# Transposes grouped, layer 2's products regrouped, and a new written-out order, in a kernel of attention and two feed-forward layers

## The chip, the cores and the metric

One core of one Trainium2 chip runs the whole kernel. The metric is device time in microseconds (us) of one execution; lower is better. Engine names are those of the profile: PE is TensorE's matmul, PEld its weight load, DVE VectorE, ACT ScalarE, POOL GpSimd, and SP the SyncE queue, which here issues all DMAs.

## What is computed

The reference, cut to its core:

```python
q, k, v: (4, 8, 576, 64) fp32;  w_in: (512, 2048), w_out: (2048, 512), twice, fp64
q_d, k_d, v_d = means over 4 neighbouring tokens of q, k, v
out_up  = repeat(softmax(q_d @ k_d.T / 8) @ v_d, 4 times along tokens)
scores  = where(|i - j| < 4, q @ k.T / 8, -1e9)
x = (out_up + softmax(scores) @ v)  reshaped to (2304, 512)
h = x @ moe_w_in;   x = (h * sigmoid(h)) @ moe_w_out
h = x @ moe2_w_in;  out = (h * sigmoid(1.702 * h)) @ moe2_w_out
```

## The kernel before

The two feed-forward layers are most of the work. Weights and activations are split into a high and a low fp16 half, and each matrix product is the sum of three products of halves. The weights come from memory as fp64 in 1 MB and 0.5 MB pieces and are converted on the way: ACT (L323, L327, L344), DVE (L331, L336, L348) and for some pieces POOL (L348) put the bits together, a sum on PE with ones (L557) and DVE reductions give a common scale, and ACT (L376, high half) and DVE (L380, low half) write the fp16 halves.

**Attention** runs in 32 units: 8 half batches m of 288 tokens, 4 pairs of heads each. A unit needs k and q with the head dimension on partitions, and their means over 4 tokens. For half batches 0 and 1 both are made on PE: for every 96 tokens `keys_of.tr` (L1128, L1129; once per batch and head pair, six chunks) and `unit.qtr` (L1173, L1174; once per unit, three chunks) issue a transpose (96 columns) and a product with the matrix `four` (24 columns, the means). That is 4 calls of 6 pairs and 8 calls of 3 pairs, 48 pairs. The other half batches use DVE for it. Then come the scores (L1198 pooled, L1204 local), the softmax on DVE, ACT and POOL (L1212 to L1256), the product with v (L1280, L1286), ACT's copy `us` (L1292) and DVE's addition into `xf` (L1300, L1301), which frees the PSUM banks of the product for the next use.

**Layer 1** takes 288 tokens at a time (L702 up, L819 and L847 down). **Layer 2** takes nine tiles of 256 tokens. A tile has eight steps p = 0 to 7 (gate pairs), each with 24 matmuls of 256 columns (L881) and, behind it, tanh on ACT (L893), a multiplication on DVE (L896), three sums (L900 to L902, on DVE or POOL), the high half on ACT (L906) and the low half on DVE (L909). Then 168 matmuls (L960) form seven products of sums of g and sums of weights. `PARTS` cuts each product into ranges of p: a part (product, p0, p1) issues three matmuls for each p, and needs both halves of g of its last p.

**What sets the order.** The code adds 2663 steps to a plan, each with its engine and what it depends on. `PLACES`, a string of two digits per step, gives each step a place, `Plan.placed` sorts by it, and each engine, and the DMA queue, issues its steps in that order. `ON` names the steps that go to another engine than their usual one: conversion steps (`sg`, `cp`), the softmax's subtraction, normalisation and division (`LS`, `LN`, `DN`), and layer 2's three sums (`gs2.tile.p`).

Of the kernel before, what the change touches and what calls it, by code (L numbers as in the profile page):

```python
# [36 lines left out]
def on(name, usual):  # L37
# [12 lines left out]
    "2l2x2B2p2F2I2K2L2O2R2S2W353d3n3h444w66828A2n1X2V3S2P2U2X37313c383b3k3m3u3r3v3K3H3O3X4041333f3j3y3t3D3z3J3L3P3T42464d4n4v4C4N5K43474b4i"  # L50
    "4m4o4r4y4B4H4O4R545g5h5m5w5z5C4Q4X505b5c5i5k5o5q5s5y5x5F5H5E5L5U5W5X63656A6Z768sai2G3E6148324u7s4U527B8b6f7d8o6r5R3Q3V4j5f5l5Y6n6b6s6o"
    "6x6z6B6H6F6J6T6P7e7n7t9k494c5B5N5Q6D6X6L776Y7l7v7C7M7J7N7Z7W81878c8z5T6g8j6V7w7z7P7L7U8d8f8m8n8u8r8x8H8F8K8Q8T927S7Y8O7p7x8h8B8l8D8q8v"
    "8I8L8N8R8W908X9497989b9p9u9y9Cac9FeM72858J9v8G939a9h9f9l9i9o9G9J9O9K9S9Wa9abafalbM8V8Z9w9Q9N9Z9R9Va3a5a8a7aqaCaNaOaTb1bV9maoasaAavaKaz"
    "aQaSaUaWb0b5bcaXbvbGbKbOaxaEb3b6bjb9brbtbwbybAbCbPbRbNbUbXbYbZc3c9cbchcPeoja6Q9Eag9n7XcCd3aMaFcYe9bLbxdmcHboaDbnbEb4bic0c6c5cac7cccfcg"
    "cjcmcDcOcxcVd7d9fCbqcucUbebgcycFcIcKcNcQcTcXdId6djdldLdQdUdXe3bscMdfcwczdgdqdudHdvdKdNe4e5eaedele7eCeGeIfscicldEcZd2e6egerenevexezeAeB"
    "eEeLePeDeTeXeZf0fJfNfPfTg8hXm5dceue0fbdAdCf1f4f6f9fafdfefgflfqfwfzfofYg5gcgZf8fufvfBfEfGfHfMfSfUfVfZgggjgmgEh0h3jhg0g3gfghgqgzgwgBgGgN"
    "h6gPhHhKhxhWi2i5i8gTgXh8hkhihMhmhnhPhThZi9ieihibikiuiwiMjujyjAjPjRkMjEdsfhg6gdejifgSh1gKjzitiXfRkGiWkHj4fFfKhoilioiyiDiEiLiIiJiQiRjliZ"
    "jijOk8kakgkhm1fxiVjrhrhvjejmjIjWjLjMk1k3k7ktkxkIkNl1lbldlehtjZkwj9jbkrkDkykOkPkWkYkZlWlmlwlAlYm6mdmemJl4lhlXkmkvlplGlslLlvlJlOlSlUm2mi"
    "mlmhmmmomqmLmNmVngnknMogrrjGkqlTlFkTkUmvmxmEmzmKmRmUn4njndnrnLnDnTo3odpRlulInnnsnynNnEnVnXokoqonozoKotoRoYp5qln3o7ofowouoDoEoHoJoOp6oU"
    "papopeprpPpTq9oQoTp8pbpfpkpjpqpsptpVpFpXq0q8qbqfqhqiqmqsqtqvqGquqw393w3M3Y4E4J3F3W4a4f4l4T4k4A4K4P4V4Z4F4S5d5j5p5v575e5r5G5P685t5S646l"  # L60
    "6v7k6e6k6C6G898e6t6w6I6S7G7R6O6W7f71797o7i7r7A7E7I807O7V8i868a8t8k8p8C8y8E8M8P8Y95999c9L969d9q9t9x9A9j9r9z9D9Haa9B9I9P9T9Ya19M9Ua2a6ay"
    "aHa0a4adajamapaeakaratawbaauaBaIaLaVb8aGaJaPb2cncJaRaYbubzbDddb7bbbhbpbBbHbQbWc1c4c8ceckcpcscGcLcScRcWd5dedhdwd4dadidndOdSdkdtdydDdFdR"
    "dxdBdMdPebepdGdJdWe1efekdTe2e8eceYf2eeemeteweReVeqeyeQfffih7eFeNeWf3f7fcfjfrgpfyfDfLfQg4gagigrgygxgAgHgRgUhhgLgQh2h5hchfgWh4h9hdhuhEhb"
    "hghlhphshYhjhqhyhAhDiihwhChIhLhQhUhJhNi0i3ivj0hSi1imiHjwjFi7igisiBiGiNiUj1jcj6j8jjjojvjBjJjNjSjQjTjVjXk0kijUjYk6k9kokQk4keklkpkKl0kjkz"
    "kFkJkRlgkEkLkVl2lBlCkSkXl3l7l9lql6lalillmYnflfljlHlRmDmHlrlylElKlQlVm0m3m8mcmjmnmsmwmCmImMmPmOmSn2n7nbnBn0n6nhnmnInQncninqnwnCo0ntnAnH"
    "nJocoenGnKnSnZo1opnOnYo4o5o8oBo2o6ohojoIoMoboioSoZpmqaomoroAoGoLoWp3pcpppipnpvpzpDpHpKpOq2pUpZq5q6qgqkq4q7qcqdqpqyqeqjqoqqqCqOqnqrqBqD"
    "qKqMqAqEqIqLqRqUqJqNqQqSqVr4qPqTr1r6rDrJqZr5rGrLrTswrbrfrjrorurxrCrKrPrNrVs1s6s7sascsgslsjspstsusxsDsssvsEsGsJsNsCsIsMsPsQsSsLsOsUsXsY"
    "tcsRsVt1t2t9tesZt3t6tatdtht5tbtgtltptttwtytDtAtEtGtItKtNtQtTtY6p8g91aZbdbfblbm8U9s9e9XahbkcobJ8S9gbSctbTd0dbdpbFcdc2cqcrcvcAcBanbId8dV"
    "dzdZeHesd1dodreJeieOeUeScEeKehfkf5fIg7fOdYfmfAftfWg1gCgnfpgbfXgkgegogugvfng9glgFgtgJgYhag2gOgDhzgVhBhOhFgsgMi6hViaidizijgIhei4hRiniriP"
    "iAhGipiCiFiKiOjdiSiciTixj3j2j5jtjDiqiYjfjgjkjnjxjqjsjKk2kdkcknkulPj7jCjpjHkbkfkskkkAl8lcm7ltmbmfmgkClkl5lnlolzlNlDmkmtmrmumymBmFmGmamp"  # L70
    "mQn1n5n9nenulMmTmWmXmZnlnznpmAnxoanRolosoxoyn8nFnonUnPnWoNoCnanvp0p4p7p9pxpdoooFoPoVoXp2pLphpgpypupBpApEpJq1plpIpMpNpQpSrhpWp1pwpGqXr3"
    "r7r9raq3rgrkrnrmrwryrzpYrerdrirlrsrArBkBqxqzqWr2ovqFqHr0rqlxqYr8rcrMk5rprtrvrHrErFrIrOrQrRrSs8sis9sbrZsHsKtftorXsTt4sWt0rWtitrtntJrUsd"
    "sosqt7tOtRueulsntutztMtPtStWu7ubtstBtFtHtLtVtZu0u3t8tqtvtxtCu2u6uZv3tUm9rYs0s2s3s5sesksBpCs4sfshsyvcvesAszm4smsrtjtkwcwYtmu9lZsFuYv7vq"
    "y2yqyswIo9v9vavkvmxZzEzwwuvnvpwewHy9zZBlBnCsx0x2xQyvzyBdBhA3DQvryazmzCzDChE3A2CJybB3DkF8FaFcFhFgFftXu1u5uaugumuqu4u8udufuiupusucuhukuo"
    "uwuAuGujunutuvuxuEuHuruuuzuBuDuKuTuyuCuIuLuOuSuWuFuJuNuPuRuVv0uMuQuXv1v5v8vduUv2v4v6vbvfvhvgvjvivlvovtvsvuvwvvvxvzvyvKvMvAvBvNx6vCvDvF"
    "vGvIvPvTvEvHvLvOvRvVw0vJvQvUvWvYw2w7vSvXw1w3w5w9whvZw4w8wawdwiwlw6wbwgwjwnwqwvwfwkwowpwswwwywmwrwxwzwBwDwFwtwAwCwEwGwJwLwKwNwMwOwPwRwQ"
    "wSwUwTwVwXwWx3x5wZx1xayWx4x7x9xbxdxgxlx8xcxfxhxjxnxsxexixmxoxqxuxzxkxpxtxvxxxBxHxrxwxAxCxExIxLxyxDxGxJxOxRxVxFxKxNxPxTxWxYxMxSxXy0y3y5"
    "y7xUy1y4y6y8ycyeydygyfyhyiykyjylytymynypyoyRyVyryuzfAaywyxyzyAyCyKyNyyyByEyFyHyXz0yDyGyJyLyPyTyYyIyMyQyUz2z9zdyOySz3z4z8zizoyZz1z5z7za"
    "zczgz6zbzhzkzlzpzrzezjzqzszuzxzAznztzvzzzBzFzHzGzJzIzKzLzNzMzOA4zPzQzSzRA6A8zTzUAOAQzVzWzYA0A5AcAgzXA1A9AbAeAiAnA7AdAhAjAlApAuAfAkAoAq"
    "AsAwACAmArAvAxAzADAGAtAyABAEAJAMARAAAFAIAKANASAUAHALATAVAXAZB1APAWAYB0B2B4B6B5B8B7B9BaBcBbBeBgBfBiBkBjCiClBmBoBtDIBpBqBsBuBwBzBEBrBvBy"  # L80
    "BABCBGBLBxBBBFBHBJBNBSBDBIBMBOBQBUC0BKBPBTBVBXC1C4BRBWBZC2C7CaCdBYC3C6C8CbCeCgC5C9CfCkCmCoCqCcCjCnCpCrCtCvCuCxCwCyCzCBCACCDECDCECGCFCI"
# [1438 lines left out]
```

## Time and profile before

| | |
|---|---|
| three runs | 901.15, 902.54, 902.81 us; median 902.54 |
| profiled execution | 902.26 us, of which the span is 900.5 us |
| PE busy | 864.3 us (96% of the span) |
| PEld busy | 717.7 us (80%) |
| DVE busy | 623.0 us (69%) |
| ACT busy | 464.0 us (52%) |
| POOL busy | 150.3 us (17%) |
| mean granted clock | 0.996 |

The profile shows one execution. Busy time counts what an engine spends in instructions; its idle time is put down to the releaser that came last. 1.76 us of the execution's own time lie outside the span. Line numbers are those of the kernel before; in the changed kernel the same lines stand up to 5 further on.

### The profile page before, as it was taken

How to read it: one execution, taken by the hardware profiler on the slowest of the kernel's cores; microseconds unless marked ns; L12 is line 12 of the kernel's file. 1: busy time of each engine (PE TensorE's matmuls, PEld its weight loads, DVE VectorE, ACT ScalarE, POOL GpSimd, SP SyncE). 2: the span in 40 equal slices, each digit the busy share in tenths (PEclk: the TensorE clock that was granted, in tenths of full speed). 3: DMA queues.
4: the chain of work that ended last, by engine and by line, in shares of the span. 5: the costliest groups of instructions: out<-in, count | busy, mean ns of one | idle time of the engine just before them, and what ended most of it. 6: DMA issues, size and time to landing. Idle time of an engine off the chain costs nothing.

```text
span 900.5 us, 23832 instructions
## 1 busy us (share of the span) xinstructions
PE 864.3 (96%) x10212; PEld 717.7 (80%) x10212; DVE 623.0 (69%) x1365; ACT 464.0 (52%) x820; POOL 150.3 (17%) x165
## 2 busy tenths in 40 slices
...
GB/s 269 204 241 230 190 63 113 69 89 127 120 118 155 150 104 98 121 106 84 129 13 293 66 41 1 12 1 24 1 25 1 36 1 13 1 36 1 25 13 36
DMA packets 116190, 77.04 MB, mean 86 GB/s; under 512 B 94836, under 2 KB 101492, under 8 KB 115060
## 3 DMA queue, kind: packets, MB, share of 16 engines
...
## 4 chain that ended last, share of the span: by engine, by line
PE 66%; DVE 25%; ACT 4%; issue 2%; DMA 2%; SPq 0%; ACTq 0%; DVEq 0%
PE hps L702 18%; PE ops L819 16%; PE oy L960 8%; DVE g L909 7%; PE hps L881 6%; PE oz L960 4%; DVE tg L896 4%; DVE tg L901 2%; PE ox L960 2%; PE ops L847 2%; DVE tg L900 2%; PE ul L1286 2%; DVE tg L902 2%; PE sl L1204 2%; DMA kraw<-in_k_dram 1%
## 5 line engine op out<-in xcount | busy, mean ns | idle before, releaser
L702 PE MATMUL hps<-xhl,win 128*128 128x288 f16 x1536 | 197.9, 288 | 0.0
L881 PE MATMUL hps<-xhl,win 128*128 128x256 f16 x1728 | 191.0, 273 | 0.2 <-DVE tg L896 0.2
L881 PEld LDWEIGHTS <-win 128*128 128x128 f16 x1728 | 168.9, 98 | 20.5 <-issue 0.6
L702 PEld LDWEIGHTS <-win 128*128 128x128 f16 x1536 | 148.9, 99 | 37.8
L819 PE MATMUL ops<-g,wout 128*128 128x288 f16 x1344 | 170.8, 287 | 0.0
L960 PEld LDWEIGHTS <-g 128*128 128x128 f16 x1512 | 146.6, 98 | 25.5 <-DVE g L909 6.5
L819 PEld LDWEIGHTS <-wout 128*128 128x128 f16 x1344 | 129.8, 98 | 32.8 <-issue 0.6
L893 ACT ACTIVATE tg<-hps,blk 128x512 f32<-128x512 f32 x72 | 49.3, 685 | 136.9 <-PE hps L881 128.8
L896 DVE SCALAR_TENSOR_TENSOR tg<-tg,hps 128x512 f32<-128x512 f32 x72 | 49.1, 682 | 54.6 <-ACT tg L893 54.6
L906 ACT ACTIVATE g<-tg 128x896 f16<-128x896 f32 x72 | 67.6, 944 | 32.1 <-DVE tg L902 30.6
L909 DVE SCALAR_TENSOR_TENSOR g<-tg,g 128x896 f16<-128x896 f32 x72 | 78.3, 1094 | 7.5 <-ACT g L906 7.2
L960 PE MATMUL oy<-wout,g 128*128 128x256 f16 x648 | 75.1, 273 | 0.3 <-DVE o L944 0.3
L714 ACT ACTIVATE tg<-hps,blk 128x576 f32<-128x576 f32 x64 | 47.1, 737 | 45.7 <-PE hps L702 37.4
L900 POOL TENSOR_TENSOR tg<-tg 128x128 f32<-128x128 f32 x9 | 6.8, 755 | 368.9 <-DVE tg L896 368.9
L717 DVE SCALAR_TENSOR_TENSOR tg<-tg,hps 128x576 f32<-128x576 f32 x64 | 47.7, 746 | 27.4 <-ACT tg L714 27.0
L348 POOL TENSOR_TENSOR cs<-cs,cz 128x512 int32<-128x512 int32 x32 | 43.0, 1346 | 134.1 <-DVE cz L336 87.6
L727 DVE SCALAR_TENSOR_TENSOR g<-tg,gs,g 128x576 f16<-128x576 f32 x56 | 47.0, 847 | 6.4 <-ACT g L724 6.3
L724 ACT ACTIVATE g<-tg,gs 128x576 f16<-128x576 f32 x56 | 42.8, 769 | 15.8 <-DVE tg L717 15.7
L938 ACT ACTIVATE o<-oy,blk 128x256 f32<-128x256 f32 x27 | 12.7, 471 | 53.8 <-PE oy L960 53.8
L323 ACT ACTIVATE st<-st 128x512 f32<-128x512 f32 (+1 forms) x48 | 39.0, 824 | 1.2 <-DMA st<-in_moe_w_out_dram 0.8
L944 DVE SCALAR_TENSOR_TENSOR o<-oy,blk,o 128x256 f32<-128x256 f32 x9 | 4.4, 484 | 47.5 <-PE oy L960 24.4
L1234 ACT ACTIVATE pd<-sl,nm 72x144 f32<-72x144 f32 x64 | 23.4, 369 | 24.1 <-DVE sc L1219 11.8
...
## 6 DMA issues: line engine op xcount, KB each, us to landing
...
```

The source lines that it names most:

```text
L348: eng.tensor_tensor(out=s, in0=s, in1=zget(), op=ALU.add)
L702: nc.tensor.matmul(o, T[w][:, kc, a, fc * P:(fc + 1) * P], T[xk][:, kc, b, :T_], start=(n == 0), stop=(n == 3 * KC - 1))
L714: ACT.activation(out=T[tg], in_=T[ps][:, :, :T_], func=AF.Tanh, scale=T["a" + bk][:, c:c + 1])
L717: DVE.scalar_tensor_tensor(out=T[tg], in0=T[tg], scalar=1.0, in1=T[ps][:, :, :T_], op0=ALU.add, op1=ALU.mult)
L727: DVE.scalar_tensor_tensor(out=T[g][:, 1], in0=T[tg], scalar=gs, in1=T[g][:, 0], op0=ALU.mult, op1=ALU.subtract)
L819: nc.tensor.matmul(o, w[:, j, a, dc * P:(dc + 1) * P], g[:, b, j % 2, :], start=(n == 0), stop=(n == 3 * NF - 1))
L881: nc.tensor.matmul(o, T[w][:, kc, a, fc * P:(fc + 1) * P], T[xk][:, kc, b, :], start=(n == 0), stop=(n == 3 * KC - 1))
L893: ACT.activation(out=four(), in_=T[ps][:, 0, :], func=AF.Tanh, scale=T["a" + bk][:, c:c + 1])
L896: DVE.scalar_tensor_tensor(out=four(), in0=four(), scalar=1.0, in1=T[ps][:, 0, :], op0=ALU.add, op1=ALU.mult)
L906: ACT.activation(out=T[g][:, 0], in_=T[tg], func=AF.Copy, scale=GS2)
L909: DVE.scalar_tensor_tensor(out=T[g][:, 1], in0=T[tg], scalar=GS2, in1=T[g][:, 0], op0=ALU.mult, op1=ALU.subtract)
L960: nc.tensor.matmul(T[bank[acc]], g[:, a, slot, :], w, start=first and p == p0 and i == 0, stop=prod in (2, 3, 4) and p == NF // 2 - 1 and ...
```

## The change

It has four parts.

1. In `keys_of.tr` and `unit.qtr` all transposes of a call come first and all products with `four` behind them. No instruction is added or removed.
2. `PARTS` puts pairs 0 to 3 of products 1, 5 and 2 first, and pairs 4 to 6 of products 1 and 5 behind them.
3. `PLACES` is another order for all 2663 steps, the DMA issues among them, and `ON` another choice of engines. Of the conversions, `cp1.in.0.2`, `cp1.in.3.2` and `cp1.out.3.0` move from POOL to DVE and `cp1.out.0.2` from DVE to POOL; `sg` goes to DVE for seven pieces instead of four; `DN` goes to ACT for 27 units instead of 15; layer 2's three sums go to POOL 19 times of 72 instead of 9.
4. The tile `dg` of a reduction helper takes an existing buffer, and a scratch tile of ACT is halved (1024 to 512 columns).

```diff
 ON = {
-    "POOL": ("cp1.in.0.2 cp1.in.3.2 cp1.out.0.0 cp1.out.1.0 cp1.out.1.2 cp1.out.2.0 cp1.out.2.2 cp1.out.3.0 cp1.out.3.2"),
...
+    "POOL": ("cp1.out.0.0 cp1.out.0.2 cp1.out.1.0 cp1.out.1.2 cp1.out.2.0 cp1.out.2.2 cp1.out.3.2"),
...
 PLACES = (
-    "0006020804070x030A1C0V1d2b1k050d111o2e010j0h0w0m0L0T090y1a0J1f0P1r0b0Z0M1315181l0c0U12101m1c20171L1N1P1V1U2c1I2g2r2m2y2s2C2j2M2Q2Y2Z30"
+    "0007020103080c050q1g0J161T1k060g0Y1y1V090v0B0K0Q0P120e0H100M150T1d040s1e0S1h131l0y1m1p1q1r1s1B0V1C1x1G1F1I211v2328292A2d2C2i2W30353e38"
...
         def a():
-            T["dg" + nm] = pools["at"].tile([P, NC, P], F32, tag="dg", name="dg", bufs=1)[:, :n]
+            if n > 1:
+                T["dg" + nm] = pools["st"].tile([P, 512], F32, tag="cs", name="cs", bufs=2).rearrange("p (n e) -> p n e", n=n)
+            else:
+                T["dg" + nm] = pools["at"].tile([P, 1, P], F32, tag="dg", name="dg", bufs=1)
...
-            junk = pools["st"].tile([P, 1024], BF16, tag="junk", name="junk", bufs=1)
+            junk = pools["st"].tile([P, 512], BF16, tag="junk", name="junk", bufs=1)
...
-    PARTS = ((1, 0, 4), (1, 4, 7), (5, 0, 4), (5, 4, 7), (2, 0, 4), (1, 7, 8), (5, 7, 8), (2, 4, 6), (6, 0, 4), (6, 4, 8), (3, 0, 4), (3, 4, 8),
+    PARTS = ((1, 0, 4), (5, 0, 4), (2, 0, 4), (1, 4, 7), (5, 4, 7), (1, 7, 8), (5, 7, 8), (2, 4, 6), (6, 0, 4), (6, 4, 8), (3, 0, 4), (3, 4, 8),
              (7, 0, 4), (7, 4, 8), (2, 6, 8), (4, 0, 4), (4, 4, 8))
...
             for c in range(2 * NBL):
                 nc.tensor.transpose(T[kps][:, c // NBL, (c % NBL) * TT:(c % NBL + 1) * TT], kr[:, c], T["ident"][:TT, :TT])
+            for c in range(2 * NBL):
                 nc.tensor.matmul(T[kps][:, c // NBL, HALF + (c % NBL) * QB:HALF + (c % NBL + 1) * QB], kr[:, c], T["four"][:TT, 0], start=True, stop=True)
...
             for c in range(NBL):
-                qr = T[f"qraw{u}"][:TT, c * 2 * D:(c + 1) * 2 * D]
-                nc.tensor.transpose(T[qps][:, c * TT:(c + 1) * TT], qr, T["ident"][:TT, :TT])
-                nc.tensor.matmul(T[qps][:, HALF + c * QB:HALF + (c + 1) * QB], qr, T["four"][:TT, 1], start=True, stop=True)
+                nc.tensor.transpose(T[qps][:, c * TT:(c + 1) * TT], T[f"qraw{u}"][:TT, c * 2 * D:(c + 1) * 2 * D], T["ident"][:TT, :TT])
+            for c in range(NBL):
+                nc.tensor.matmul(T[qps][:, HALF + c * QB:HALF + (c + 1) * QB], T[f"qraw{u}"][:TT, c * 2 * D:(c + 1) * 2 * D], T["four"][:TT, 1], start=True, stop=True)
```

**SP, the first DMAs of the program.** `st` is a raw piece of weights (1 MB), `kraw`, `qraw`, `vraw` and `vw` are pieces of k, q and v. Before:

```order
L518 DMA st_169<-in_moe_w_in_dram 128x2x1024
L1049 DMA kraw<-in_k_dram 96x6x64 x2
L1049 DMA qraw<-in_q_dram 96x3x64 x4
L1049 DMA kraw<-in_k_dram 96x6x64 x2
L1061 DMA vraw<-in_v_dram 72x4x256
L518 DMA st_195<-in_moe_w_in_dram 128x2x1024
```

Now:

```order
L1065 DMA vraw<-in_v_dram 72x4x256
L1053 DMA kraw<-in_k_dram 96x6x64 x2
L1053 DMA qraw<-in_q_dram 96x3x64 x2
L522 DMA st_177<-in_moe_w_in_dram 128x2x1024
L1053 DMA qraw<-in_q_dram 96x3x64 x2
L1053 DMA kraw<-in_k_dram 96x6x64 x2
L522 DMA st_195<-in_moe_w_in_dram 128x2x1024
```

The first piece of k stood behind a piece of weights; it now stands behind a piece of v, and the weights behind k and q.

**DVE, around the second unit's addition into `xf`** (the second group of L1300 and L1301, L1305 and L1306 now; `win` are finished weights, L348 and L349 a conversion). Before:

```order
L380 SCALAR_TENSOR_TENSOR win_0_545<-x_80,bin_88,win_0_545 128x2x512
L1219 TENSOR_TENSOR sc<-sl,cap 128x192
L1222 TENSOR_REDUCE mx<-sc 128x6
L1212 TENSOR_REDUCE nm<-sl 72x2
L1228 TENSOR_TENSOR sc<-sc,mx 128x192
L380 SCALAR_TENSOR_TENSOR win_1_580<-x_80,bin_88,win_1_580 128x2x512
L1300 TENSOR_TENSOR xf<-ul_547,us 128x3x24
L1300 TENSOR_TENSOR xf<-ul_548,us 128x3x24
L1301 TENSOR_TENSOR xf<-ul_549,us 128x2x3x24
```

Now:

```order
L349 ISA x_80<-x_80,z 128x2048
L1224 TENSOR_TENSOR sc<-sl,cap 128x192
L1227 TENSOR_REDUCE mx<-sc 128x6
L332 TENSOR_SCALAR x_80<-st_388 128x1024
L284 TENSOR_SCALAR wi_101<-wi_101 128x1
L285 TENSOR_SCALAR ibin_87<-wi_101 128x1
L286 RECIPROCAL bin_88<-ibin_87 128x1
L1305 TENSOR_TENSOR xf<-ul_555,us 128x3x24
L1305 TENSOR_TENSOR xf<-ul_556,us 128x3x24
L1306 TENSOR_TENSOR xf<-ul_557,us 128x2x3x24
L1217 TENSOR_REDUCE nm<-sl 72x2
L381 SCALAR_TENSOR_TENSOR win_1_607<-x_80,bin_88,win_1_607 128x2x512
```

The addition was behind the low half of `win_1`; now it is ahead of it.

**DVE, the end of layer 2's last tile** (L896 and L900 are the multiplication of a pair, L909 and L913 the low half of g). Before:

```order
L909 SCALAR_TENSOR_TENSOR g<-tg,g 128x896 x2
L944 SCALAR_TENSOR_TENSOR o<-ox,blk,o 128x256
L896 SCALAR_TENSOR_TENSOR tg<-tg,hps 128x512
L900 TENSOR_TENSOR tg<-tg 128x128
L901 TENSOR_TENSOR tg<-tg 128x2x128
L902 TENSOR_TENSOR tg<-tg 128x128
L909 SCALAR_TENSOR_TENSOR g<-tg,g 128x896
```

Now:

```order
L913 SCALAR_TENSOR_TENSOR g<-tg,g 128x896
L900 SCALAR_TENSOR_TENSOR tg<-tg,hps 128x512
L904 TENSOR_TENSOR tg<-tg 128x128
L905 TENSOR_TENSOR tg<-tg 128x2x128
L906 TENSOR_TENSOR tg<-tg 128x128
L913 SCALAR_TENSOR_TENSOR g<-tg,g 128x896 x2
L754 TENSOR_TENSOR blk<-blk,osc_99 128x1
```

Before, the low halves of pairs 5 and 6 came first (the two rows in one), then all of pair 7. Now the low half of pair 6 stands behind pair 7's sums, so that it and pair 7's low half end the tile; the same holds in all nine tiles.

## Rows read from the trace of the kernel before

**Rows 1.** Busy time by stretch: start:end, length, busy time (instructions) per engine, granted clock, DMA share, GB/s.

```profile
0.00:25.00 25.00, 15.18 (x178) 13.79 (x178) 7.92 (x24) 12.13 (x26) 5.39 (x28) 1.00 1.03 262
25.00:75.00 50.00, 36.91 (x604) 32.01 (x604) 44.31 (x94) 40.11 (x66) 14.58 (x11) 1.00 0.96 236
75.00:150.00 75.00, 70.44 (x1179) 54.34 (x1177) 71.55 (x181) 60.73 (x112) 34.54 (x27) 0.95 0.56 133
150.00:525.00 375.00, 374.25 (x4942) 294.55 (x4940) 267.61 (x636) 206.42 (x421) 76.69 (x74) 1.00 0.44 116
525.00:901.00 376.00, 367.49 (x3318) 322.98 (x3316) 231.60 (x434) 144.64 (x197) 19.08 (x27) 1.00 0.04 14
```

**Rows 2.** PE's waits: line <- releaser: us in total, times, longest.

```profile
PE kps L1128 <- DMA kraw<-in_k_dram: 7.5, 1, 7.5
PE sps L557 <- DVE x L331: 5.2, 3, 2.8
PE kps L1128 <- DVE xf L1301: 3.7, 1, 3.7
```

**Rows 3.** Timeline of PE, the start: start us, us, what [idle before].

```profile
8.02 0.40 PE L1128 MATMUL kps<-ident,kraw 96*128 96x96 f32 x1
8.22 0.52 PE L1129 MATMUL kps<-four,kraw 96*128 96x24 f32 x2
8.56 0.40 PE L1128 MATMUL kps<-ident,kraw 96*128 96x96 f32 x1
...
68.20 2.87 PE L702 MATMUL hps<-xhl,win 128*128 128x288 f16 x12
```

**Rows 4.** Chain of waits, 25 to 35 us: four transposes of 72 columns.

```profile
31.31 0.48 PE tps L1263 x4
```

**Rows 5.** Timeline of DVE, 34 to 50 us.

```profile
41.48 1.74 DVE L380 SCALAR_TENSOR_TENSOR win<-x,bin,win 128x1024 f16<-128x1024 f32 x1
...
43.43 0.29 DVE L1301 TENSOR_TENSOR xf<-ul,us 128x144 f32<-128x144 f32 x1
...
47.09 2.28 DVE L348 CUSTOM_DVE_ANT_0 x<-x,z 128x2048 uint16<-128x2048 uint16 x1
```

**Rows 6.** Timeline of ACT, 41 to 44 us.

```profile
41.86 0.39 ACT L1292 ACTIVATE us<-ul 128x288 f32<-128x288 f32 x1
```

**Rows 7.** Timeline of PE, layer 1: a wait, the matmuls behind it, and later ones.

```profile
127.31 0.47 PE L1198 MATMUL sl<-kd,qd 64*72 64x144 f32 x4 [1.62 <-DVE qd L1187]
...
128.26 4.78 PE L847 MATMUL ops<-g,wout 128*128 128x288 f16 x24
...
193.81 3.11 PE L819 MATMUL ops<-g,wout 128*128 128x288 f16 x24
```

**Rows 8.** Timeline of PE, layer 2's tile 2, its first products.

```profile
636.05 2.73 PE L960 MATMUL oy<-wx,g 128*128 128x256 f16 x21
638.62 2.46 PE L960 MATMUL oz<-wout,g 128*128 128x256 f16 x21
...
642.22 0.49 PE L960 MATMUL oy<-wx,g 128*128 128x256 f16 x3
```

**Rows 9.** PEld's waits, 530 us to the end.

```profile
PEld L960 <- DVE g L909: 6.5, 13, 0.8
PEld L960 <- issue: 1.6, 7, 0.5
```

**Rows 10.** Timeline of DVE, the end of tile 2's gates.

```profile
636.25 2.19 DVE L909 SCALAR_TENSOR_TENSOR g<-tg,g 128x896 f16<-128x896 f32 x2
638.36 0.68 DVE L896 SCALAR_TENSOR_TENSOR tg<-tg,hps 128x512 f32<-128x512 f32 x1
...
641.16 1.09 DVE L909 SCALAR_TENSOR_TENSOR g<-tg,g 128x896 f16<-128x896 f32 x1 [1.01 <-ACT g L906]
```

**Rows 11.** Layer 2's first sum by engine: duration ns min/median/max, first and last start.

```profile
L900 DVE TENSOR_TENSOR tg<-tg x63: 283/292/642, 540.0 to 881.1; 128x128 f32<-128x128 f32 x63
L900 POOL TENSOR_TENSOR tg<-tg x9: 452/454/1436, 538.2 to 860.9; 128x128 f32<-128x128 f32 x9
```

More of the change, by code (lines that the diff above doesn't have):

```diff
@@ L50 @@
[L50 to L81, printed above, removed]
@@ new lines @@
+    "3m262I3n2N3t3c3K0Z181a1u1j1o1A1H1L1S2x2G2j2l2D2O2M2Z3j3l3q4X4h4r2r3f3k3p3v3s3H402E3z3Q3N4G4i4o5a3A4u4M4E5g505f5E3G4H4V4S5r5v5y5P3U4Z5z"
+    "5m5L5X62635l615U6e6o6z6H6F5T6r716X7g797e7p5V6M7B6U7G787j7O4q4v6b6j6g6m5O6i6D766T726V6Z7m7x7s7F7E7K7P847V818R0b0f0a0d0h0i0m0k0r0l0o0t0u"
+    "0C0z0D0F0N0X14191b0n0w0x0j0p0A0G0E0L0I0O0R0U110W1c1f171D1J1M251n1t1O1i1w1z1N1E1Q1K1R1X1Y1Z202b2f272g2q2t2w1P1W2o1U22242c2e2h2k2n2p2s2v"
+    "2u2y2B2z2F2H2J2K2P2T2U343a2X2Y3S3J517d7h8u2a2m2R3L2L2Q2S36323b373d3i3r3x3y3D3M3E3P3Y415831393o3B3w3I3C3O3R3T3X3Z484f4a4w4D4J5M45494d4m"
@@ new lines @@
+    "4j4p4n4y4A4B4K4F4N4Y5d5i5o5t5u4O4T4W565259575e5j5k5q5w5A5F5x5K5Q5S60656t6x7b7k88aU2V335Y4I3g4t6v55427I695J7J8l6N7A3V444e5G5I5Z6c676l6f"
+    "6k6p6u6C6A6G6R7i7l7q7t8H4c5D5s5B5N6B6S6L776Q747f7o7v7z7L857Q868c8k945h5p8b6a6K7H7U7R827Z8f8g8j8o8m8z8C8K8O8T8V8X8h8s8x8q8r8y8E8A8J8F8M"
+    "8P8Q8Z8U8Y9192979f9i9k9o9H9Ja2af9VdO708v8e95899e9m9q9s9u9t9A9C9D9S9G9L9Oa6acahakc893989z9M9P9X9ZaaadaAaQaCaFaOaVaZb6bbbTa3a5aqaIaBaKaE"
+    "aTaXaYb4b1biblb9bGbKbNbOb3bfbjbnbobsbtbybzbBbDbHbPbSbQbUbWbYc5cmcqcIcLcWecj6au8Daian8natbkb7bwcJbLbpcfe0e3cMbdbEajaSbMc2c4c9cgcbcecjcl"
@@ new lines @@
+    "ctcpcscDcHcNcQd0d9cackcdc0c6coczcvcFcxcRcScVdgcXd8dtdodxdBdDeEcrcCdTcwcEdbdjdfdndidkdGdIdRdQdWeje8eneueBeLdwdyegd4d5dFdXdUe2e6elepeseD"
+    "eweFeIeHeMeOeQeReWeYflftfDgfhgcyd6effXe9ebeSf3f1f5f8fbfefffgfhfnfqfjfNfTfWgFemerfcfyfmfEfrfHfJfKfLfMg5g9fQgqgwgygOeZfafZgbg2gigcgpgCgU"
+    "gVh3hbhihshAhHhJhLgjgmgKhhgNhmgPgShqhrhthIhNhRhOhUhZi3i7injejgjYkgkMkUeqhzgBfFdziRiNgtf9jUjCidgkkhjIjLi2f7fOiIg6gaieigikihiqisiCiGiYiJ"
+    "iSjOjGjTkckmkoggimjyi0i6iBjij3jljcjdjrjtjJjxkAkEjRkOkXkZl3gQkpk9iwiykwkGkIkKkJkPkRkSl9lwlBlFlulMlQlUlXjbk8lGjnl1lilnlylHlAlDlJlKlRlTlW"
```

36 lines of the change are left out of this document (28 added, 8 removed), and 15 rows, old and new, of the table ON.

## The prediction

> **What bounds the kernel now.** I read the busy times by stretch first [rows 1]. The reader is to see where PE is idle: in the first 150 us it works 122.5 of 150 us (15.18 + 36.91 + 70.44), from 150 to 525 us 374.25 of 375, from 525 us to the end 367.5 of 376. So PE sets the pace, and all that can be won without removing matmuls is 27.5 us at the start and 8.5 us in layer 2 and the tail. In the start PE is not alone in being busy: the DMA engines are full for 75 us (shares 1.03 and 0.96), and DVE works 115.9 of the 125 us from 25 to 150 (44.31 + 71.55). A gain there must pass through these two as well.
>
> Next, PE's waits [rows 2]: 7.5 us for the first piece of k, 5.2 us in three waits for converted weights, 3.7 us once for the addition into `xf`. Then the timeline of the start, where transposes and products alternate [rows 3]; the first matmuls of layer 1 begin at 68.20 us. Last, the first products of a layer 2 tile [rows 8], where idle time is hidden inside merged rows: 21 matmuls with `oy` take 2.73 us and 21 of the same shape with `oz` right behind take 2.46. The weight loads show who is late: PEld waits 6.5 us in 13 places for the low half of g, and 1.6 us in 7 more [rows 9].
>
> **The change part by part.** The sum is made against the profiled execution's 902.26 us; the median of the runs, 902.54, is 0.3 above it, so a forecast against one holds for the other.
>
> *First DMAs.* Ahead of the first piece of k stood 1.05 MB of weights; now 0.29 MB of v stands there. At the 262 GB/s of that stretch [rows 1] the 0.76 MB less are 2.9 us. The bounds are 0 (if the time to the first landing does not depend on what is ahead) and 2.9. I take 2.5, since PE's wait [rows 2] is for this one transfer, and the engines are full. The weights lose what k gains: by the first three weight pieces about the same 4.3 MB have gone out either way, so the 5.2 us for converted weights stay.
>
> *Grouping.* No instruction goes away; only the alternation does. A pair takes 0.54 us (8.02 to 8.56): 0.20 from the transpose's start to the product's, 0.34 from there to the next transpose [rows 3]. In a run of four, a transpose of 72 columns takes 0.12 [rows 4], so 0.16 for 96 columns. For the product in a run there is no row; at best it takes what the transpose's interval is, 0.20, at worst so much that the pair stays at 0.54. So a pair gains between 0 and 0.18 us. I take 0.08, in the middle, as nothing in the trace tells which. Of the 48 pairs, 42 lie ahead of 68.20 us (24 of k, 18 of q; the other 6 are at full clock and short). That is 3.4 us of PE time, at most 7.6. It counts only where PE is not about to wait for weights anyway. I take half: 1.7, at most 3.8. If PE's loads of weights, which stay the same, set the pace, it is 0.
>
> *The addition into `xf`.* PE waited 3.7 us for it. On DVE it stood behind a low half of weights of 1.74 us that began at 41.48 [rows 5]; ACT's copy `us`, which it also needs, was done at 42.25 [rows 6], while the low half ended at 43.2. Without that low half ahead the addition could begin 0.9 us sooner. More is possible only if `us` is sooner too, and in the new order `us` stands behind other conversions. What is late next is thus `us`. Bounds 0 and 1.2; I take 0.9.
>
> *What this adds to DVE.* Two conversions of up-weights come from POOL. One takes 2.28 us on DVE [rows 5], together 4.6, in a stretch in which DVE has 9.1 us free (125 - 115.9). The conversion of weights is what layer 1's matmuls wait for, so some of it is paid; I take half, 2.3. Bounds 0 (all of it falls into DVE's free time) and 4.6. The swap of one conversion of down-weights for another costs nothing net. Divisions moved to ACT ease DVE a little after 75 us, where ACT is busy 60.7 of 75 us and has the room; I count nothing for it. The smaller scratch tile and the `dg` tile change no instruction's length.
>
> So at 150 us the kernel should be 2.5 + 1.7 + 0.9 - 2.3 = 2.8 us ahead, and since PE is full from there to 525 us, the gain goes through, unless DVE's or the queue's later work turns out late. I count nothing for that, and keep it in the first rival.
>
> *Layer 2.* After the last h matmul of a tile PE has 18 products (pairs 0 to 3, 4 and 5 of product 1) before it needs pair 6; at 0.11 us each (2.46 for 21, its tail included) that is 2.0 us. The low half of pair 6 ends 2.4 us after the products' start in tile 2 (636.25 + 2.19 = 638.44, against 636.05) [rows 8, 10]. Now 42 products stand ahead of it, 4.6 us. The low half of pair 6 itself moves behind pair 7's multiplication and sums, 0.68 + 1.0 us, so it ends near 4.1: in time, with 0.5 us to spare. Pair 7 is asked for after 54 products both ways, 5.9 us. Its low half now ends 6.2 us after the start (641.16 + 1.09 = 642.25), and on DVE 1.0 us of that is a wait for ACT [rows 10], which the new order fills with pair 6's low half; it should end near 5.2. So both waits can go. Of 6.5 + 1.6 us [rows 9] I take 5.5, since the spare is thin and part of the 1.6 is other work. Bounds 3 (pair 6 in time, pair 7 late in most tiles) and 7.
>
> Sum: 902.26 - 2.8 - 5.5 = 893.96, so **894 us**.
>
> **Rivals.**
>
> *1. The start's gain does not arrive.* DVE and DMA, not PE, set when the first weights are ready. For it: the shares of 1.03 and 0.96, DVE's 115.9 of 125 us, and that two more conversions go to DVE. Against it: the 7.5 us for k is a wait for one transfer, and everything of attention hangs on it. Then layer 2 alone gains: 902.3 - 5.5 = 896.8, up to 899 if a new wait in the middle takes 2 us more.
>
> *2. All of it arrives.* Start 2.9 + 3.8 + 1.2 = 7.9, DVE's new work hidden, layer 2 6.5: 887.9.
>
> *3. POOL's sums come late.* POOL now does the sums of 19 gate pairs instead of 9. On POOL the first sum takes 0.45 us at the median but 1.44 at the longest, on DVE 0.29 [rows 11]. So a trio is sometimes about a microsecond later, as long as one low half on DVE. Pair 6's sums go to POOL in two tiles (1 and 4); 1.0 us for the long sum and about 0.6 for POOL's pace, less the 0.5 to spare, is 1.1 us each, 2.2 in all: 896.2. The Trainium skill ("SBUF — State Buffer", section "SBUF: two separate sides") has a rule that speaks against this part of the change: DVE and GpSimd share a port pair as an exclusive lock, held for a whole instruction, which a DVE operation with two SBUF inputs takes against a GpSimd operation that reads SBUF. By that rule each of the 19 trios could be held up, or hold DVE up; the trace agrees in that the longest sum is 0.98 us over the median (1436 against 454 ns), but most of the nine were not held up.
>
> *4. Slower.* In layer 1 a wait costs more than its length: after a wait of 1.62 us 24 matmuls took 4.78 us where later ones of that shape take 3.11 [rows 7], 1.67 more, and the granted clock of 75 to 150 us is 0.95 [rows 1]. If each of the two added conversions on DVE becomes a wait of PE of its own 2.28 us there, with such a stretch behind it, they cost 2 x (2.28 + 1.67) = 7.9; and if those waits are set by the arrival of weights, the start gains nothing. Less layer 2's 5.5: 902.3 + 2.4 = 904.7. It decides from more than 5.5 us of added waits with their slow stretches, that is two over 1.1 us each. For it: DVE's load. Against it: 9.1 us free on DVE, and the first piece of k comes sooner whatever DVE does.
>
> That the grouping does nothing at all is no rival of its own: it takes 1.7 us off the gain (895.7).
>
> **How the numbers follow.** Forecast 0.50, rival 1 0.25, rival 2 0.10, rival 3 0.08, rival 4 0.07. The forecast's own range, from its terms' bounds, is 890 to 898. For 8 times in 10 the range has to take in most of rival 1, rival 3, and the upper part of rival 2: 889 to 899.5; left out are rival 4 (0.07) and the ends of rivals 1 and 2 and of the forecast (0.11). A measurement of this kernel can tell about 0.2%, 1.8 us, from no change. Faster by more: 0.50 + 0.20 + 0.10 + 0.06 = 0.86. Within: 0.07, the ends of rivals 1 and 3. Slower: 0.07, rival 4.
>
> **What would show it.** PE's first transpose near 5.0 us instead of 7.50; six transposes of k in one row of less than 1.2 us; the first L702 (L706 then) near 63 to 65 us instead of 68.20; PE busy near 73 of the 75 us after it; and in layer 2 PEld's wait for g near 1 us instead of 6.5, with `oy` and `oz` parts of equal length. Wrong would be: the first layer 1 matmuls at 68 us or later, new waits of PE above 1.5 us between 75 and 150 us or in the middle, or layer 2's wait for g still above 4 us.

## The result

The changed kernel takes 893.62 us (median of four runs, 892.67 to 895.12); the kernel before, on the same chip, 901.97 (four runs). The ratio is 0.9915, interval 0.9901 to 0.9928: 0.85% faster, 8.35 us by the medians, and 893.62 against the 894.0 forecast. The profiled execution is the lowest of the four, 892.67, with a span of 890.9 us, and the two traces differ by 9.6 us (900.5 against 890.9), 1.2 more than the medians.

The busy times by stretch, in the form of [rows 1]:

```profile
0.00:25.00 25.00, 16.04 (x178) 14.46 (x178) 7.73 (x23) 11.69 (x25) 8.04 (x30) 1.00 0.98 252
25.00:75.00 50.00, 44.15 (x693) 37.38 (x692) 46.26 (x110) 42.87 (x74) 10.08 (x11) 1.00 1.01 237
75.00:150.00 75.00, 68.20 (x1120) 52.90 (x1120) 69.59 (x171) 57.20 (x104) 29.25 (x23) 0.98 0.62 147
150.00:525.00 375.00, 374.86 (x4941) 295.31 (x4940) 265.65 (x626) 212.72 (x445) 73.48 (x67) 1.00 0.42 114
```

From 25 to 75 us PE works 44.15 us instead of 36.91. From 75 to 150 us it works 2.2 us less. Not all of that is given back: the granted clock there is 0.98 instead of 0.95, and at a lower clock the same work counts as a longer busy time. The middle is full as before. PE's waits, as in [rows 2]:

```profile
PE kps L1132 <- DMA kraw<-in_k_dram: 6.1, 1, 6.1
PE tps L1268 <- ACT pd L1256: 3.5, 2, 2.4
PE ops L851 <- DVE g L731: 2.1, 1, 2.1
...
PE sps L561 <- DVE x L332: 1.7, 3, 1.2
```

The wait for k fell from 7.5 us only to 6.1. The three waits for converted weights fell from 5.2 to 1.7, and the wait of 3.7 us before a call of k's transposes is gone. New are a wait of 2.4 us for a division on ACT (at 109 us) and one of 2.1 us for layer 1's gates (at 137 us). Behind the first of them 48 matmuls of layer 1 take 7.71 us, where 48 of that shape take 6.04 later; the last section shows the rows. The timeline of PE, as in [rows 3]:

```profile
6.12 1.20 PE L1132 MATMUL kps<-ident,kraw 96*128 96x96 f32 x6 [6.12 <-DMA kraw<-in_k_dram]
7.11 2.65 PE L1134 MATMUL kps<-four,kraw 96*128 96x24 f32 x12
9.58 0.72 PE L1177 MATMUL qps<-ident,qraw 96*128 96x96 f32 x3
...
63.76 3.08 PE L706 MATMUL hps<-xhl,win 128*128 128x288 f16 x12
```

Six transposes take 0.99 us (6.12 to 7.11), 0.165 each, but six products 2.47 (7.11 to 9.58), 0.41 each. The call takes 3.46 us where the alternating one took 3.19 (7.50 to 10.69). In this stretch grouping is a loss. Layer 1 still begins 4.44 us sooner (63.76 against 68.20), and layer 2 4.0 us sooner (528.9 against 532.9).

In layer 2, tile 2's products on PE, as in [rows 8]:

```profile
631.27 1.47 PE L964 MATMUL oy<-wx,g 128*128 128x256 f16 x12
...
635.43 1.15 PE L964 MATMUL oy<-wx,g 128*128 128x256 f16 x9
636.41 1.15 PE L964 MATMUL oz<-wout,g 128*128 128x256 f16 x9
637.39 0.49 PE L964 MATMUL oy<-wx,g 128*128 128x256 f16 x3
```

the low halves of pairs 6 and 7 on DVE (timeline, as in [rows 10]):

```profile
634.52 1.08 DVE L913 SCALAR_TENSOR_TENSOR g<-tg,g 128x896 f16<-128x896 f32 x1
...
635.62 1.09 DVE L913 SCALAR_TENSOR_TENSOR g<-tg,g 128x896 f16<-128x896 f32 x1
```

and PEld's waits there, as in [rows 9]:

```profile
PEld L964 <- issue: 0.8, 5, 0.2
PEld L964 <- DVE g L913: 0.5, 1, 0.5
```

Pair 6's half ends 4.3 us after the products' start (635.60 against 631.27) and PE comes to it about 4.8 us after it; pair 7's ends at 5.4 and is asked for at 6.1. Parts of equal size take equal time. From its first h matmul to the end of the last product layer 2 takes 358.4 us instead of 364.0 (the expectations below count to the start of the last product: 358.1 and 363.7). This length repeats where layer 2 is the same: 358.4 us in the changed kernel and in e1, e8, e11 and e12 below, 363.9 to 364.0 in the kernel before, e2 and e7. So differences of it of 1 us and more can be read from single traces.

### The profile page after: what moved, and what is told of

It reads as the page before. It is cut to its first block, busy times and chain, and to the rows that moved or that the text cites. A ratio compares the mean times of both kernels' runs of the same rounds, so it can differ in the third digit from the quotient of the medians.

```text
span 890.9 us, 23880 instructions
## 1 busy us (share of the span) xinstructions
PE 864.1 (97%) x10212; PEld 721.5 (81%) x10212; DVE 608.9 (68%) x1334; ACT 470.4 (53%) x841; POOL 160.8 (18%) x187
## 4 chain that ended last, share of the span: by engine, by line
PE 84%; DVE 11%; ACT 2%; issue 1%; DMA 0%; SPq 0%; DVEq 0%; ACTq 0%
PE ops L823 19%; PE hps L706 18%; PE hps L885 18%; PE oy L964 10%; PE oz L964 5%; PE ox L964 3%; PE ul L1291 2%; PE sl L1209 2%; PE ops L851 2%; DVE g L913 1%; PE sl L1203 1%; PE ul L1285 1%; DVE wout L381 1%; PE tps L1268 1%; PE kps L1134 1%
## 5 line engine op out<-in xcount | busy, mean ns | idle before, releaser
L885 PE MATMUL hps<-xhl,win 128*128 128x256 f16 x1728 | 190.4, 273 | 1.3 <-DVE tg L900 1.3
L885 PEld LDWEIGHTS <-win 128*128 128x128 f16 x1728 | 169.1, 98 | 21.2 <-issue 1.6
L964 PEld LDWEIGHTS <-g 128*128 128x128 f16 x1512 | 147.7, 98 | 18.6 <-issue 0.8
L900 DVE SCALAR_TENSOR_TENSOR tg<-tg,hps 128x512 f32<-128x512 f32 x72 | 49.1, 682 | 53.1 <-ACT tg L897 53.1
L913 DVE SCALAR_TENSOR_TENSOR g<-tg,g 128x896 f16<-128x896 f32 x72 | 78.1, 1097 | 0.6 <-ACT g L910 0.3
L904 POOL TENSOR_TENSOR tg<-tg 128x128 f32<-128x128 f32 x19 | 15.1, 793 | 341.9 <-DVE tg L900 341.9
L964 PE MATMUL oy<-wout,g 128*128 128x256 f16 x648 | 75.1, 272 | 0.0
L349 POOL TENSOR_TENSOR cs<-cs,cz 128x512 int32<-128x512 int32 x32 | 43.9, 1378 | 149.0 <-DVE cs L332 67.7
```

Of the source, the lines that this page charges most:

```text
L349: eng.tensor_tensor(out=s, in0=s, in1=zget(), op=ALU.add)
L885: nc.tensor.matmul(o, T[w][:, kc, a, fc * P:(fc + 1) * P], T[xk][:, kc, b, :], start=(n == 0), stop=(n == 3 * KC - 1))
L900: DVE.scalar_tensor_tensor(out=four(), in0=four(), scalar=1.0, in1=T[ps][:, 0, :], op0=ALU.add, op1=ALU.mult)
L913: DVE.scalar_tensor_tensor(out=T[g][:, 1], in0=T[tg], scalar=GS2, in1=T[g][:, 0], op0=ALU.mult, op1=ALU.subtract)
L964: nc.tensor.matmul(T[bank[acc]], g[:, a, slot, :], w, start=first and p == p0 and i == 0, stop=prod in (2, 3, 4) and p == NF // 2 - 1 and ...
```

## The experiments

All twelve use the same two kernels as starting points. Ratios are to the kernel before, timed on the same chip. Line numbers are those of each run's own kernel.

**e1: the changed kernel, grouping undone.**

```diff
-            for c in range(2 * NBL):
                 nc.tensor.matmul(T[kps][:, c // NBL, HALF + (c % NBL) * QB:HALF + (c % NBL + 1) * QB], kr[:, c], T["four"][:TT, 0], start=True, stop=True)
...
-            for c in range(NBL):
                 nc.tensor.matmul(T[qps][:, HALF + c * QB:HALF + (c + 1) * QB], T[f"qraw{u}"][:TT, c * 2 * D:(c + 1) * 2 * D], T["four"][:TT, 1], start=True, stop=True)
```

> The changed kernel with its grouping alone undone: transposes and products with `four` alternate again, every place in the order kept. Theory (grouping costs PE time): in the trace of the changed kernel a grouped call of k takes 3.46 us from its start to the next work (6.12 to 9.58) where the alternating one took 3.19 (7.50 to 10.69), and a call of q 1.73 against 1.61. So undoing it should take 4 x 0.27 + 6 x 0.12 = 1.8 us off PE's work ahead of layer 1, of which about 1 us arrives: first layer 1 matmul near 62.7 us instead of 63.76, time near 892.6 against 893.6. Rival (the start is set by DMA and DVE, PE's pairs are hidden): first layer 1 matmul unchanged within 0.3 us, time the same. The prediction's own term (grouping gains 1.7): first layer 1 matmul 1 to 2 us later, time near 895.

893.62 us, ratio 0.9914 (0.9901 to 0.9928): no different from the changed kernel.

**e2: the kernel before, grouping alone** (the same lines the other way).

> The kernel before with the grouping alone. Theory (grouping costs): each call of k 0.27 us and each of q 0.12 longer, first layer 1 matmul at 68.7 to 70 us instead of 68.20, time 0.5 to 1.8 us above the kernel before. The prediction's term: 1.7 us below it. Rival (hidden): the same within 0.5 us.

902.60 us against 901.39, ratio 1.0013 (1.0004 to 1.0022): 1.2 us slower. Its layer 1 begins at 69.40 us, 1.2 later, and ahead of it PE's work itself is longer. The busy times up to the first layer 1 matmul, in one fence for each: the kernel before,

```profile
0.00:68.20 68.20, 45.45 (x684) 41.01 (x685) 45.70 (x98) 45.47 (x78) 18.41 (x36) 1.00 0.99 237
```

with the grouping alone (e2),

```profile
0.00:69.40 69.40, 47.14 (x685) 42.71 (x685) 45.30 (x99) 45.63 (x78) 19.31 (x36) 1.00 0.93 233
```

the changed kernel,

```profile
0.00:63.76 63.76, 48.95 (x692) 43.44 (x693) 42.96 (x103) 43.67 (x81) 14.37 (x37) 1.00 1.01 245
```

and the changed kernel with alternation (e1).

```profile
0.00:63.76 63.76, 47.32 (x693) 41.72 (x694) 43.46 (x103) 43.65 (x81) 14.57 (x37) 1.00 1.00 251
```

The grouping adds 1.69 us of PE work in one (47.14 - 45.45) and 1.63 in the other (48.95 - 47.32), near the 1.8 worked out from single calls. Before, 1.2 of it arrive in the time. In the changed kernel none does: e1's layer 1 begins at the same 63.76. Its k came 0.34 us later (6.46 against 6.12), and PE's idle time grew from 14.8 to 16.4 us (63.76 - 48.95, 63.76 - 47.32). There, other waits take what the alternation saves: besides the one for k, those for converted weights take 3.0 us instead of 1.7.

**e3: the kernel before, products' order alone.**

```diff
-    PARTS = ((1, 0, 4), (1, 4, 7), (5, 0, 4), (5, 4, 7), (2, 0, 4), (1, 7, 8),
+    PARTS = ((1, 0, 4), (5, 0, 4), (2, 0, 4), (1, 4, 7), (5, 4, 7), (1, 7, 8),
```

with these parts' places exchanged to match.

> The kernel before with the new order of layer 2's products alone (pairs 0 to 3 of products 1, 5 and 2 first); DVE, ACT, POOL and SP issue exactly what they did. Theory A (the order of the products gives most of layer 2's gain): PEld's wait for the low half of g falls from 6.5 us to 2 or less, layer 2 from its first h matmul to the last product takes 4 to 5 us less than 363.7, time near 897.5. Theory B (it is pair 7 that then makes PE wait, since its low half still ends about 6.2 us after the products' start and is asked for at 5.9; the new order of the gates on DVE is needed too): 1 to 3 us less, time near 900.

901.20 us against 901.39, ratio 1.0002 (0.9992 to 1.0012): nothing. Layer 2 takes 364.2 us. PEld's waits there:

```profile
PEld L960 <- issue: 4.2, 10, 1.5
PEld L960 <- DVE g L909: 3.2, 7, 1.0
```

and PE's:

```profile
PE oz L960 <- DVE o L944: 1.4, 1, 1.4
PE oy L960 <- DVE g L909: 1.2, 4, 0.7
...
PE ox L960 <- DVE o L944: 0.8, 3, 0.3
```

The wait for g halves, from 6.5 to 3.2, but new ones come for `o`, DVE's additions of finished products, which free the accumulators. All of PEld's waits in the products together hardly change, 7.7 us (3.2, 4.2 and 0.3 for ACT) against 8.1 (6.5 and 1.6). Both named releasers are DVE's, whose order was made for the old products. Neither theory said how little this part brings: A's amount fell, and B named only pair 7.

**e4: the changed kernel, old products' order** (the reverse of e3's edit).

> The changed kernel with the old order of layer 2's products; all other engines issue what the changed kernel's do. Theory A (products' order alone): 4 to 6 us slower than the changed kernel, near 898.5. Theory B (both belong together): pair 6's low half now stands behind pair 7's sums on DVE, so with the old order PE waits for it 1 to 2 us in each of nine tiles: 9 to 18 us slower, 903 to 912, slower than the kernel before.

917.84 us, ratio 1.0177 (1.0148 to 1.0205): 24 us slower than the changed kernel, more than theory B's upper end. Tile 2 on PE:

```profile
639.05 0.82 PE L964 MATMUL oy<-wx,g 128*128 128x256 f16 x6
640.18 0.39 PE L964 MATMUL oy<-wx,g 128*128 128x256 f16 x2 [0.31 <-ACT g L910]
641.91 0.28 PE L964 MATMUL oy<-wx,g 128*128 128x256 f16 x1 [1.34 <-DVE g L913]
```

It waits here for a high half on ACT and then 1.34 us for a low half on DVE. In all (PE's waits):

```profile
PE oy L964 <- DVE g L913: 16.0, 12, 2.4
```

Layer 2 takes 383.3 us, 24.9 more than in the changed kernel. 17.0 of them are idle time of PE, within theory B's 9 to 18; the other 7.9 are longer busy time for the same number of matmuls. Part of that is the clock: the granted clock is 0.97 to 0.99 from 520 to 750 us, where the changed kernel's is 1.00. Theory B had the waits right and no term for this. In this kernel the new order of the gates fits only the new products.

**e5: the kernel before, layer 2's whole new order.** The edit of e3, and all steps behind layer 2's first h step in the changed kernel's order on PE, DVE and ACT; no step changes its engine. In outline, with g0 for a pair's multiplication, gs for its sums and gl for the low half of g:

```diff
 # DVE, the end of each tile
-gl.5 gl.6 g0.7 gs.7 gl.7
+gl.5 g0.7 gs.7 gl.6 gl.7
```

> The kernel before with the whole new order of layer 2 on PE, DVE and ACT (behind its first h step; products and gates), and nothing else: the choice of engines, POOL, SP and layer 1 stay. The products' order alone gained nothing, so theory B (products and gates together, no need of POOL's ten more sums): layer 2 from its first h matmul to the last product takes 4.5 to 6 us less than 363.7 (the changed kernel: 358.1), time near 896. Theory C (the sums moved to POOL are needed too, since DVE is what is late at a tile's end): 0 to 2.5 us less, near 900.

897.85 us against 900.93, ratio 0.9962 (0.9949 to 0.9975): 3.1 us, between the theories. Layer 2 takes 361.2 us, 2.8 less. What is left, on PEld and then on PE:

```profile
PEld L881 <- issue: 3.5, 4, 1.2
PEld L960 <- DVE g L909: 2.0, 4, 0.8
```

```profile
PE hps L881 <- DVE tg L896: 2.8, 3, 1.0
```

PE still waits for DVE, now mostly for the multiplications that free the PSUM banks of h.

**e6: the changed kernel, layer 2's order undone** (old products, and pairs 4 to 7 in the old order on DVE and ACT; POOL's sums stay).

> The changed kernel with the old order of the products and the old order of gate pairs 4 to 7 within each tile on DVE and ACT; the rest, POOL's sums too, stays. Theory B: layer 2 takes 4 to 7 us more than 358.1, time 898 to 900.5, nearer to what the start alone leaves (893.6 + 5.6 = 899.2). Theory C: the same 4 to 7 us minus what POOL's sums bring, 895 to 898.

910.35 us, ratio 1.0115 (1.0085 to 1.0144): 17 us slower than the changed kernel; both theories were far off. PE's waits:

```profile
PE oy L964 <- DVE g L913: 6.3, 10, 2.0
...
PE oy L964 <- ACT g L910: 3.6, 4, 1.8
```

Layer 2 takes 375.0 us, 16.7 more than in the changed kernel: 10.0 of idle time of PE and 6.7 of longer busy time (granted clock 0.97 to 0.98 in part of it). All four waits for ACT lie in tiles 1, 3 and 4, which have 12 of POOL's 19 pairs; that ACT is late there because it waits for POOL's sums is a reading of that and was not tried. The run is no clean undoing of layer 2, and tells only that engines and order fit one another; e10 is the clean one.

**e7: the kernel before, the first piece of k first.**

```diff
-L518 DMA st_169<-in_moe_w_in_dram 128x2x1024
 L1049 DMA kraw<-in_k_dram 96x6x64 x2
+L518 DMA st_169<-in_moe_w_in_dram 128x2x1024
```

> The kernel before with the first piece of k's DMA ahead of the first 1 MB of weights, and nothing else. PE's first transposes should begin 1.5 to 3 us before 7.50. The prediction's term (2.5 us of it reach layer 1): first layer 1 matmul near 65.7 to 66.7 instead of 68.20, time near 899.5. Rival (a later wait, for converted weights, absorbs it, since their transfers end when they did): first layer 1 matmul 68.2 within 0.5, PE's wait for converted weights (L557) 1.5 to 3 us longer than 5.2, time the same.

900.61 us against 900.93 (ten runs, 897.82 to 902.25), ratio 0.9989 (0.9976 to 1.0001): not told from no change. PE's waits:

```profile
PE sps L557 <- DVE x L331: 5.7, 3, 2.8
PE kps L1128 <- DMA kraw<-in_k_dram: 4.2, 1, 4.2
```

PE begins 3.3 us sooner, and in this profile (898.16, among the lowest of its ten runs) layer 1 begins at 65.73, 2.5 sooner, as the prediction's term had it. In the median only 0.3 us are left. The ten runs are spread wide: three lie at 897.8 to 898.2, below every run of the kernel before (lowest 900.03), so in some the gain arrives. Where it goes in a median run no profile shows.

**e8: the changed kernel, two conversions back on POOL.**

```diff
-    "POOL": ("cp1.out.0.0 cp1.out.0.2 cp1.out.1.0 cp1.out.1.2 cp1.out.2.0 cp1.out.2.2 cp1.out.3.2"),
+    "POOL": ("cp1.in.0.2 cp1.in.3.2 cp1.out.0.0 cp1.out.0.2 cp1.out.1.0 cp1.out.1.2 cp1.out.2.0 cp1.out.2.2 cp1.out.3.2"),
```

> The changed kernel with the two conversions of up-weights that went to DVE (cp1.in.0.2 and cp1.in.3.2) back on POOL. The prediction's term (they cost 2.3 us on DVE): PE 1 to 3 us further at 150 us, time near 891.5. Rival 1 (they fit into DVE's idle time): the same within 0.7. Rival 2 (the conversion is on the way to the first weights, and POOL takes longer for it than DVE): first layer 1 matmul 0.5 to 3 us later than 63.76, time 894 to 897.

894.16 us, ratio 0.9923 (0.9907 to 0.9938), against the changed kernel's 0.9915: not told apart. In its profile, the slowest of its four runs (895.30), layer 1 begins 0.5 us later (64.28) and layer 2 2.6 later (531.6); 1.67 of that is a stretch at the lower clock that the changed kernel's profile does not have (last section). If the two conversions cost 2.3 us, the ratio would be near 0.989, outside the interval. The term by which these conversions cost DVE 2.3 us falls.

**e9: the changed kernel, POOL's sums as before** (9 gate pairs on POOL instead of 19; the `gs2` names of `ON` exchanged).

> The changed kernel with layer 2's sums on the engines of the kernel before (9 gate pairs on POOL instead of 19), every place kept. Theory C (ten more sums on POOL are a part of layer 2's gain, since DVE is late at a tile's end; the order of layer 2 alone brought 2.8 of 5.6 us in the trace): layer 2 takes 2 to 3.5 us more than 358.1, time 895.5 to 897. Theory B (order only): within 0.7 us of the changed kernel. The prediction's rival 3 (POOL's sums are late): 0.5 to 2.2 us faster.

894.84 us, ratio 0.9932 (0.9920 to 0.9944): the median 1.2 us above the changed kernel's, with intervals that overlap. Layer 2 takes 360.4 us, 2.1 more. The exchange shifts line numbers by 5 (L880 and L959 are the changed kernel's L885 and L964); PEld's waits:

```profile
PEld L880 <- issue: 2.5, 4, 1.1
PEld L959 <- DVE g L908: 2.0, 4, 0.8
```

The wait for g is what e5 had left. The times alone do not tell this run from the changed kernel; the length of layer 2 does.

**e10: the kernel before with all of layer 2's change** (e5, and the changed kernel's `gs2` names).

> The kernel before with all of the change's layer 2: the order of products and gates, and the choice of engines for the sums (19 on POOL). Layer 1 and its start stay as before. Theory C: layer 2 near 358 us as in the changed kernel, time near 895.5 (5.5 us below the kernel before), so that the start is worth only about 2. Theory B: no better than the order alone, near 897.9.

895.82 us against 901.17, ratio 0.9948 (0.9935 to 0.9960): 5.35 us. Layer 2 takes 359.3 us, 4.7 less than before and 0.9 more than the changed kernel, and PEld's wait for g is that of the changed kernel (L955 is the L960 of before):

```profile
PEld L955 <- DVE g L904: 0.5, 1, 0.5
```

So by the ratios layer 2 is worth 0.52%, and layer 1 with its start the other 0.33% of the change's 0.85, about 3 us (1.3 to 4.6 by the two intervals), rather than the 2 expected here. That the start does gain, the traces bear out: layer 2 begins at 531.1 to 533.8 us in the kernel before, e3, e5 and e10, and at 528.5 to 529.0 in the changed kernel, e4, e6 and e9.

**e11 and e12: the first piece of k ahead of the first piece of v**, in the changed kernel, alternating (e11) and grouped (e12).

```diff
-L1065 DMA vraw<-in_v_dram 72x4x256
 L1053 DMA kraw<-in_k_dram 96x6x64 x2
+L1065 DMA vraw<-in_v_dram 72x4x256
```

> A version that could beat both: the changed kernel with alternating transposes and products, and the first piece of k ahead of the first piece of v in the DMA queue. PE's first transposes at 4.2 to 5.2 us instead of 6.1; first layer 1 matmul at 61.8 to 62.8 instead of 63.76. If what is won there arrives: time near 892. If later waits absorb it, as in the kernel before with k first: 893.3 to 893.9.

> The changed kernel, grouped as it is, with the first piece of k ahead of the first piece of v. PE's first transposes at 4.2 to 5.2 us. If grouping costs what it did alone in the kernel before (1.2 us): 1 us behind the version that alternates, near 893. If PE's time there is hidden: equal to it.

e11: 894.64 us (890.43 to 896.18), ratio 0.9921 (0.9903 to 0.9940); e12: 895.14 us, ratio 0.9936 (0.9922 to 0.9949). PE begins at 4.1 and 4.4 us, but layer 1 at 63.74 and 66.23. In e12's timeline the wait is only moved:

```profile
20.14 0.76 PE L1203 MATMUL sl<-kd,qT 64*72 64x144 f32 x4 [2.31 <-ACT kd L1139]
...
26.13 1.01 PE L561 MATMUL sps<-x,ones 128*128 128x128 bf16 x8 [1.72 <-DVE x L332]
```

Neither beats the changed kernel; no kernel here is shown to. e11's profile is of its lowest run, 890.43, the lowest of all runs here, and its six runs are spread over 5.8 us.

## Why the prediction was right

The time, 894.0 against 893.62, and the size and mechanism of layer 2's part were right. The start's sum, 2.8 us against about 3 measured, was right by luck: of its four terms one had the wrong sign, one was not there and one is not shown to be paid for, and a gain that was put at nothing, shorter waits for converted weights, is there.

*Layer 2, -5.5.* It measured -5.6 in the trace; e10, which has it alone, gives -4.7 in its trace and -5.35 in its time. The working for pairs 6 and 7 held to 0.2 us (4.1 and 5.2 forecast, 4.3 and 5.4 measured). But the split among its causes was not what the text says: the regrouping of the products alone brings nothing (e3), with the order of the gates 2.8 us in the trace (e5), and the last part comes with the sums on POOL (e5 to e10: layer 2 from 361.2 to 359.3 us in the traces). The traces of e9 and the changed kernel say the same, 2.1 us. In the times both steps have intervals that overlap (0.9962 to 0.9948, 0.9932 to 0.9915). So the step "bounds 3 (pair 6 in time, pair 7 late in most tiles)" was too kind to a partial change: a wait removed for g came back as a wait for accumulators, on the same DVE.

*Rival 3 (POOL's sums late).* Its sign was wrong. A slow sum on POOL is there, the first sum by engine as in [rows 11]:

```profile
L904 DVE TENSOR_TENSOR tg<-tg x53: 282/291/552, 536.1 to 870.7; 128x128 f32<-128x128 f32 x53
L904 POOL TENSOR_TENSOR tg<-tg x19: 452/456/1370, 536.2 to 852.0; 128x128 f32<-128x128 f32 x19
```

up to 1.37 us against a median of 0.46: eight of the nineteen take 1.23 us or more, eleven 0.45 or 0.46. The Trainium skill ("SBUF — State Buffer", "SBUF: two separate sides") has an operation of DVE with two SBUF inputs and one of GpSimd that reads SBUF exclude each other on a shared port pair; the eight agree with that, the eleven show that it does not strike every time. All the same, with ten more trios of 1.0 us off DVE layer 2 is 1.9 to 2.1 us shorter, and PEld's wait for DVE's low half of g falls from 2.0 to 0.5. So what rival 3 left out is that DVE, the engine that is late, is relieved.

*Grouping, -1.7.* Wrong in sign. The step that failed is the bound "at worst so much that the pair stays at 0.54": a product in a run takes 0.41 us, and the pair 0.165 + 0.41 = 0.577. The trace of before had no row of such products in a run, and no reason excluded a loss; the bound should have stood open above nothing. The transposes' part held (0.16 worked out, 0.165 measured). Grouping costs 1.65 us of PE work ahead of layer 1, 1.2 us of time where it was tried alone, and none in the changed kernel (e1).

*First DMAs, -2.5.* PE's wait fell by 1.4; v's piece still goes ahead, and with k first of all (e7) it fell by 3.3. A sooner k is not shown to be paid for: in the changed kernel k sooner by 1.7 and 2.1 us does not bring layer 1 forward (66.23 in e12, 63.74 in e11, against 63.76), and in the kernel before 3.3 us bring 2.5 in the profile of a low run and 0.3 in the median of ten.

*The addition into `xf`, -0.9, and weights, 0.* The 3.7 us wait is gone, with waits for `xf` of 1.4 and 0.7 in its place, and the 5.2 us for converted weights, which the text left as they were, fell to 1.7. Of 22.75 us that PE is idle ahead of layer 1 (68.20 - 45.45) 14.81 are left, while its work grew by 3.5 (45.45 to 48.95). So the start's gain lies in the new order and engines of conversions and attention as a whole; which of its moves does it was not taken apart, and stays open. The moves are more than the four parts name: the softmax's subtraction and normalisation change engine too (`LS` goes to DVE for 15 units instead of 11, `LN` for 15 instead of 13), and the prediction had no term for the three more `sg` on DVE.

*DVE's two conversions, +2.3.* Not there (e8). Part of the start's gain is given back elsewhere: of 4.44 us at layer 1's beginning 4.0 are left at layer 2's. PE has two new waits between 100 and 140 us, 2.4 for a division on ACT and 2.1 for gates. Such waits of more than 1.5 us were one of the prediction's signs of being wrong, and "PE busy near 73 of the 75 us" did not come either (68.2). Of its other signs the first transpose came at 6.12 us instead of near 5.0; those on layer 1's beginning and on layer 2 came as said.

*Rivals 1, 2 and 4* did not come true as totals: the start with layer 1 gives 4.0 us in the trace and about 3 by the ratios. But rival 4's mechanism, a new wait with a slow stretch behind it, is there once, 2.4 us and 1.67 more, from ACT's division and not from DVE's conversions.
